# Identity multiplications on TensorE ahead of the first scores and among the packing steps of batch 0

## The chip, the cores and the metric

The kernel runs on one core of a Trainium2 chip, as one program. The metric is device microseconds of one execution, lower is better; the median of three runs of the kernel before is 1284.42 us (1284.23 to 1290.81).

## The reference, cut to what matters

Attention with packed keys comes first, for 8 batches of 8 heads, 576 tokens and head size 64: 32 pack rows `p` per head attend to `k`, `v`, and then the tokens `q` attend to the 32 packed rows. After it comes a mixture of four experts over all 4608 tokens, dense, each a two-layer network with ReLU, weighted by normalised probabilities.

```python
p_packed = sm_attn(p, k, v)              # 32 pack rows against 576 keys
out = sm_attn(q, p_packed, p_packed)     # 576 tokens against 32 packed rows
x = out.transpose(0, 2, 1, 3).reshape(B * S, H * D)
p = domain_probs / (domain_probs.sum(-1, keepdims=True) + 1e-09)
for e in range(E):
    h = np.maximum(x @ w1[e], 0.0)
    out += p[:, e:e + 1] * (h @ w2[e])
```

All of it is fp32. The kernel does the large products as sums of rounded fp32 parts (a high and a low part of each operand, in a one-pass fp32 type), and the small ones of attention in plain fp32; the second expert product goes by seven block products in place of eight.

## The kernel before, in words

One batch and one half expert (512 of the hidden columns) make a unit of work, 64 units in all. Each unit has two stages: tokens times a folded first weight (packed rows times `w1`, so that attention's second product and the expert's first become one), and then seven block products with the second weight. From about the unit 2 on the program is a long, dense stream of multiplications on TensorE, with VectorE, ScalarE and GpSimd preparing operands beside it.

The head of the program has no such stream to hide in. Batch 0 is packed first, alone, in two row groups `g` = 0 and 1, each with its own generator `pack_unit` (line 144), advanced in turns by `wavefront` (line 736). A group goes through these steps: load `kt` (its keys) and then `vt`/`vr` (its values); `scores` (line 126) multiplies pack rows with keys into one PSUM tile, 8 calls in a fixed row, and then VectorE takes the maximum (line 175) and scales it (179), ScalarE takes the exponential (181), and VectorE works out the reciprocal of the sum (188, 189); five transposes turn the result (lines 198 and 199, issued by `tr` at line 74); 20 multiplications with the values (line 208, by `mm` at line 69); VectorE scales that by the reciprocal (216); one transpose (219); VectorE copies it into the block-diagonal tile `ppbd` (222). The order of program, hence of TensorE, is: scores 0, scores 1, transposes 0, transposes 1, values 0, values 1, last transpose 0, last transpose 1.

`first_tokens` (line 399) follows: 20 calls of token scores with `ppbd` (line 422), the fold of `ppbd` with four loaded quarters of `w1` (`wraw`, line 430), high and low parts of the fold on ScalarE, and then the token softmax of batch 0 on VectorE and ScalarE. It already has rows of identity multiplications at three places (`fill`, line 439, with the counts of `FILL`, line 38).

The order on each engine comes from a planner that simulates the program's times when it is built. `together` (line 76) takes it out of its hands for a list of multiplications: they stand on TensorE behind everything issued before them, in the order of the list, and everything issued later stands behind them. What `mm` and `tr` issue is free among itself between two such lists. All loads go through one queue, SP's, in the order of the program: `kt` twice, `vt` and `vr` twice, tokens, second-weight blocks, tokens, the four `wraw`, and more. An fp32 call of TensorE appears in the trace as two MATMUL and two LDWEIGHTS records, an fp32 transpose as one of each.

Of the kernel before, what the change touches and what calls it, by code (L numbers as in the profile page):

```python
# [16 lines left out]
P = 128  # L17
B, H, S, D = 8, 8, 576, 64
# [3 lines left out]
NG = NPAIR // 2  # L22
SB = B // 2
HS = S // 2
# [11 lines left out]
PLAIN = ["a11", "a12", "a21", "a22"]  # L36
NPROD = len(ORDER)
FILL = (2, 4, 3)


@with_exitstack
def attention_moe(ctx: ExitStack, tc: tile.TileContext, q, k, v, p, dp, w1, w2, out):
# [17 lines left out]
    def after(ins, prev):  # L60
        tc.add_manual_dep(ins, prev.name, nosync, reason="order on an engine")

    def on_pe(res):
        if order["last"] is not None:
            after(res.ins, order["last"])
        order["free"].append(res.ins)

    def mm(**kw):
        res = nc.tensor.matmul(**kw)  # L69
        on_pe(res)  # L70
        return res.ins

    def tr(**kw):
        on_pe(nc.tensor.transpose(**kw))  # L74

    def together(calls):

        for i, kw in enumerate(calls):
            ins = nc.tensor.matmul(**kw).ins  # L79
            for prev in order["free"] if i == 0 else []:  # L80
                after(ins, prev)
            if order["last"] is not None:
                after(ins, order["last"])
            order["last"] = ins
        order["free"] = []

    def dbl():
        return ps_dbl.tile([P, 2, 512], F32, name="dbl")

    ident = const.tile([P, P], F32, name="ident")  # L90
# [10 lines left out]
    def cols(b, hh):  # L101

        i = (hh + b) % 2
        return slice(i * NPK, (i + 1) * NPK)

    def hi_of(dst, src, eng):
        if eng is nc.scalar:
            return nc.scalar.copy(out=dst, in_=src)  # L108
        return eng.tensor_copy(out=dst, in_=src)
# [13 lines left out]
        )  # L123
        nc.scalar.dma_start(out=pnd.rearrange("e (p t) -> p e t", p=P), in_=pb)

    def scores(bs, g, stationary, moving):

        pss = {b: dbl() for b in bs}
        calls = []
        for c in range(2):  # L130
            for j in range(2):
                for hh in range(2):
                    for b in bs:
                        p0 = 2 * j * NPK + cols(b, hh).start
                        calls.append(dict(
                            out=pss[b][p0:p0 + NPK, c, 0:HS], lhsT=stationary(b, 2 * g + j, hh),
                            rhs=moving[b][hh * D:(hh + 1) * D, j, c * HS:(c + 1) * HS], start=True, stop=True,
                        ))
        together(calls)
        return pss  # L140

    pts = {}

    def pack_unit(bs, g, new, relief=False):
        nfull = S // P
        r = S - nfull * P
        kts = {}
        for b in bs:
            if g == 0:
                pts[b] = small.tile([P, NPAIR, NPK], F32, name="pt")  # L150
                nc.sync.dma_start(out=pts[b], in_=p[b])
            kts[b] = new(b, [P, 2, S], "kt")
            nc.sync.dma_start(out=kts[b], in_=k[b][:, 2 * g:2 * g + 2, :])
        yield

        def load_v(b):
            vt, vr = new(b, [P, nfull, 4 * D], "vt"), new(b, [P, 4 * D], "vr")
            nc.sync.dma_start(
                out=vt, in_=v[b, 0:nfull * P, g * 4 * D:(g + 1) * 4 * D].rearrange("(c p) d -> p c d", p=P),
            )  # L160
            nc.sync.dma_start(out=vr[0:r], in_=v[b, nfull * P:S, g * 4 * D:(g + 1) * 4 * D])
            return [vt[:, c, :] for c in range(nfull)] + [vr]

        vt = load_v(bs[0])
        yield
        pss = scores(bs, g, lambda b, pr, hh: pts[b][hh * D:(hh + 1) * D, pr, :], kts)
        a1s, rss = {}, {}
        for b in bs:
            nb = small.tile([P, 1], F32, name="nb")
            a1s[b] = new(b, [P, S], "a1")  # L170
            a1v, raw = a1s[b].rearrange("p (c s) -> p c s", c=2), pss[b][:, :, 0:HS]
            if relief:
                nc.scalar.copy(out=a1v, in_=raw)
                raw = a1v
            nc.vector.tensor_reduce(out=nb, in_=raw, axis=AX.XY, op=ALU.max)  # L175
            if relief:
                nc.scalar.mul(nb, nb, -SCALE)
            else:
                marks["bias", b, g] = nc.vector.tensor_scalar_mul(nb, nb, -SCALE).ins
            sm = small.tile([P, 1], F32, name="sm")  # L180
            marks["first", b, g] = nc.scalar.activation(
                out=a1v, in_=raw, func=AF.Exp, scale=SCALE, bias=nb, accum_out=sm
            ).ins
            rss[b] = small.tile([P, 1], F32, name="rs")
            if relief:
                nc.scalar.activation(out=rss[b], in_=sm, func=AF.Copy, bias=1e-9)
            else:
                nc.vector.tensor_scalar_add(rss[b], sm, 1e-9)
            nc.vector.reciprocal(out=rss[b], in_=rss[b])
        yield  # L190
        prs = slice(2 * g, 2 * g + 2)
        for b in bs:
            if b != bs[0]:
                vt = load_v(b)
            at = new(b, [P, len(SC), P], "at")
            ps = dbl()
            for c in range(nfull):
                tr(out=ps[:, 0, c * P:(c + 1) * P], in_=a1s[b][:, c * P:(c + 1) * P], identity=ident)
            tr(out=ps[0:r, 1, 0:P], in_=a1s[b][:, nfull * P:S], identity=ident)
            turn = nc.vector if (b, g) == (0, 0) else nc.scalar  # L200
            hi_of(at[:, 0:nfull, :], ps[:, 0].rearrange("p (c s) -> p c s", s=P), turn)
            marks["turned", b, g] = hi_of(at[0:r, nfull, :], ps[0:r, 1, 0:P], turn).ins
            yield
            ps = dbl()
            for c, (_, n) in enumerate(SC):
                for h in range(4):
                    p0 = h // 2 * 2 * NPK + cols(b, h % 2).start
                    mm(
                        out=ps[p0:p0 + NPK, 0, 0:D], lhsT=at[0:n, c, p0:p0 + NPK],
                        rhs=vt[c][0:n, h * D:(h + 1) * D], start=c == 0, stop=c == len(SC) - 1,  # L210
                    )
            ppn = small.tile([P, D], F32, name="ppn")
            if relief:
                nc.scalar.mul(ppn, ps[:, 0, 0:D], rss[b])
            else:
                nc.vector.tensor_scalar_mul(ppn, ps[:, 0, 0:D], rss[b])
            yield
            ps = dbl()
            tr(out=ps[0:D, 0, 0:P], in_=ppn, identity=ident)
            psv = ps[0:D, 0, 0:P].rearrange("p (j n) -> p j n", j=2)  # L220
            for hh in range(2):
                hi_of(
                    ppbd[b % 4][hh * D:(hh + 1) * D, prs, cols(b, hh)], psv[:, :, cols(b, hh)],
                    nc.scalar if relief else nc.vector,
                )
            yield
# [172 lines left out]
    def first_tokens(pools, qts, raws, forms, grps):  # L399
# [93 lines left out]
        spare = turned[0][:, 0, cut:cut + P]  # L493
        fill(FILL[0], spare)
        for g in range(NG):
            then("ACT", hi_of(ghls[g][:, 0, :], fold[:, g, :], nc.scalar))
            less(fold[:, g, :], ghls[g][:, 0, :])
        for g in range(NG):
            then("ACT", nc.scalar.copy(out=ghls[g][:, 1, :], in_=fold[:, g, :]))
        fill(FILL[1], spare)  # L500
        shifted(1)
        powers(1)
        parts = turn(0)
        fill(FILL[2], fold[:, 0, 0:P])
        for ts, x in parts:
# [247 lines left out]
    def drain(gen):  # L753
        for _ in gen:
            pass
# [5 lines left out]
    with ExitStack() as first:  # L761
        pools = [first.enter_context(tc.tile_pool(name=f"unit{u}", bufs=1)) for u in range(NG)]

        def unit_tile(u):
            return lambda b, shape, name: pools[u].tile(shape, F32, name=name)

        def form_tile(shape, name):
            if name == "b2":
                return st_tile(F32)[:, 0:2 * DM].rearrange("p (f d) -> p f d", f=2)
            return hpool.tile(shape, F32, name="ablk", bufs=6)  # L770

        packs = [pack_unit([0], g, unit_tile(g)) for g in range(NG)]
        forms = t_form(0, form_tile, {n: nc.gpsimd for n in ("t1", "t2", "t3", "t4")})
        norm_probs()
        for i in (0, 1, 0, 1):
            next(packs[i])
        loads = first_loads()
        qts = [next(loads)]
        next(forms)
        qts.append(next(loads))  # L780
        raws = w1_load(0)
        load_probs(0, 0)
        drain(wavefront(packs, 1))
        rest = first_tokens(pools, qts, raws, forms, ((0, 0), (0, 1), (1, 1), (1, 0)))
        raws = w1_load(1)
# [36 lines left out]
    for u, (sb, ch, b) in enumerate(units):  # L822
# [46 lines left out]
        for i in range(NPROD):  # L869
            product(u, i)  # L870
            n = i + LA
# [78 lines left out]
```

## Time and profile before

| | us |
|---|---|
| median of three runs | 1284.42 |
| the profiled execution, its own time | 1283.3 |
| its span | 1281.5 |
| TensorE busy (98% of the span) | 1259.4 |
| VectorE busy | 958.6 |
| GpSimd busy | 859.9 |
| ScalarE busy | 492.5 |
| first multiplication starts | 5.26 |

Busy times overlap, so they don't add up to the span. Times in the trace count from the start of the span; what lies around the span is 1.8 us in the profiled execution. The names PE and PEld are TensorE's multiplications and its weight loads, DVE is VectorE, ACT is ScalarE, POOL is GpSimd, SP is the queue of the loads.

### The profile page before, as it was taken

Reading aid. Unit: us, or ns where it says so; the run is one execution under the profiler, and the core shown is the slowest. Engines: PE = TensorE matmul, PEld = TensorE weight load, DVE = VectorE, ACT = ScalarE, POOL = GpSimd, SP = SyncE. Lnnn points to the kernel's source line nnn. Section 1 sums busy time; section 2 is a strip of 40 time slices with the busy share of each in tenths; the row PEclk is TensorE's granted clock in tenths of the full one; section 3 lists DMA queues with packets and bytes.
Section 4 is the critical chain, followed back from the end, with each engine's and each line's share of the span. In section 5 each row is a group of like instructions: output and inputs, shape, how many; then the busy total and the mean of one; then the engine's idle time right before and its main releaser. Section 6 shows DMA issues by size and latency. Waiting matters only on the chain.

```text
span 1281.5 us, 26882 instructions
## 1 busy us (share of the span) xinstructions
PE 1259.4 (98%) x10772; PEld 1174.3 (92%) x10772; DVE 958.6 (75%) x1302; ACT 492.5 (38%) x885; POOL 859.9 (67%) x570
## 2 busy tenths in 40 slices
PE   7999999999999999999999999999999999999998
PEld 5789998998999999999999999999999999999998
DVE  5776777899975667997777667799679567766776
ACT  3544545646334333333324423333323533332321
POOL 4878888798995554666578464476568755556565
PEclk9999999999999999999999999999999999999999
DMA  9885656544466544554355546433436443454562
GB/s 347 320 296 186 221 178 227 181 146 169 159 222 197 164 159 131 187 162 158 128 151 174 183 143 205 144 126 125 155 128 213 149 136 116 127 155 127 178 216 99
DMA packets 91707, 223.93 MB, mean 175 GB/s; under 512 B 9280, under 2 KB 32192, under 8 KB 91584
## 3 DMA queue, kind: packets, MB, share of 16 engines
q1 hardware_dynamic: 90768, 221.92, 52.2%
q8 instruction: 86, 1.41, 0.5%
q10 hardware_dynamic: 816, 0.30, 0.1%
q14 instruction: 37, 0.30, 0.1%
HBM read 183.31 MB, written 38.87 MB: 173 GB/s over the span
## 4 chain that ended last, share of the span: by engine, by line
PE 72%; POOL 12%; DVE 9%; issue 3%; ACT 2%; DMA 1%; SPq 0%; ACTq 0%; DVEq 0%; POOLq 0%
PE dbl L69 66%; POOL st L112 8%; PE dbl L79 5%; DVE sblk L582 2%; POOL acc L731 2%; DVE ghl L112 1%; DVE ablk L356 1%; DVE acc L700 1%; POOL tt L112 1%; ACT ghl L108 1%; PE dbl L74 1%; POOL xl L112 1%; POOL b L621 0%; DVE a L244 0%; DVE nb L175 0%
## 5 line engine op out<-in xcount | busy, mean ns | idle before, releaser
L69 PE MATMUL dbl<-st,tt 128*128 128x288 f32 x5388 | 766.1, 296 | 2.5 <-DVE ghl L112 1.4
L69 PEld LDWEIGHTS dbl<-st,tt 128*128 128x128 f32 x5388 | 724.7, 188 | 46.7 <-issue 24.9
L112 POOL TENSOR_TENSOR st<-sblk,st 128x576 fp32r<-128x576 f32 x252 | 398.1, 1588 | 232.8 <-ACT st L108 221.6
L69 PE MATMUL dbl<-xh,ghl 128*128 128x288 f32 x2016 | 409.2, 295 | 3.3 <-DVE ghl L112 3.3
L112 POOL TENSOR_TENSOR st<-ablk,st 128x576 fp32r<-128x576 f32 x193 | 292.4, 1519 | 139.8 <-ACT st L108 134.5
L700 DVE TENSOR_TENSOR acc<-dbl,acc 128x576 f32<-128x576 f32 x385 | 287.8, 751 | 104.5 <-PE dbl L69 103.9
L69 PEld LDWEIGHTS dbl<-xh,ghl 128*128 128x128 f32 x2016 | 322.6, 188 | 4.0 <-DVE ghl L112 4.0
L356 DVE SCALAR_TENSOR_TENSOR ablk<-dbl,pbt 128x576 f32<-128x576 f32 x256 | 192.2, 752 | 142.7 <-PE dbl L69 141.1
L69 PE MATMUL dbl<-xl,ghl 128*128 128x288 f32 x1008 | 296.7, 295 | 0.0
L108 ACT CAST st<-sblk 128x576 fp32r<-128x576 f32 x252 | 170.4, 676 | 279.9 <-DVE sblk L582 215.3
L108 ACT CAST st<-ablk 128x576 fp32r<-128x576 f32 x193 | 130.4, 676 | 256.0 <-PE dbl L69 226.1
L69 PEld LDWEIGHTS dbl<-xl,ghl 128*128 128x128 f32 x1008 | 189.1, 188 | 0.0
L582 DVE TENSOR_TENSOR sblk<-ablk 128x576 f32<-128x576 f32 x126 | 134.1, 1065 | 9.2
L108 ACT CAST ghl<-dbl 128x512 fp32r<-128x512 f32 x128 | 73.0, 588 | 112.8 <-DVE ghl L112 57.8
L112 DVE TENSOR_TENSOR ghl<-dbl,ghl 128x512 fp32r<-128x512 f32 x126 | 84.7, 687 | 20.3 <-ACT ghl L108 18.1
L582 DVE TENSOR_TENSOR sblk<-ablk,sblk 128x576 f32<-128x576 f32 x63 | 78.5, 1246 | 5.4
L79 PE MATMUL dbl<-wraw,ppbd 64*32 64x512 f32 x1024 | 69.1, 597 | 0.0
L112 POOL TENSOR_TENSOR tt<-b,tt 128x512 fp32r<-128x512 f32 x42 | 62.3, 1493 | 2.1 <-ACT tt L108 2.0
L582 DVE TENSOR_TENSOR sblk<-sblk,ablk 128x576 f32<-128x576 f32 x63 | 58.1, 923 | 1.2
L731 POOL TENSOR_TENSOR acc<-acc,acc 128x576 f32<-128x576 f32 x28 | 43.5, 1562 | 12.6 <-DVE acc L700 12.5
L698 ACT COPY acc<-dbl 128x576 f32<-128x576 f32 x56 | 35.9, 641 | 36.5 <-PE dbl L69 36.4
L79 PEld LDWEIGHTS dbl<-wraw,ppbd 64*32 64x32 f32 x1024 | 15.4, 105 | 21.4 <-issue 18.1
(115 smaller groups left out, 465.2 us busy)
## 6 DMA issues: line engine op xcount, KB each, us to landing
tt<-td SPq DMA_DIRECT2D x192, 512.0 KB, 4.3
wraw<-in_w SPq DMA_DIRECT2D x136, 256.0 KB, 3.6
td<-tt SPq DMA_DIRECT2D x56, 512.0 KB, 4.0
pbt<-pnd SPq DMA_DIRECT2D x32, 288.0 KB, 4.1
out<-acc SPq DMA_DIRECT2D x31, 288.0 KB, 2.3
kt<-in_k SPq DMA_DIRECT2D x14, 576.0 KB, 5.7
kt<-in_q SPq DMA_DIRECT2D x14, 576.0 KB, 6.2
vt<-in_v SPq DMA_DIRECT2D x15, 512.0 KB, 5.1
```

What stands on the lines that cost most here:

```text
L69: res = nc.tensor.matmul(**kw)
L74: on_pe(nc.tensor.transpose(**kw))
L79: ins = nc.tensor.matmul(**kw).ins
L108: return nc.scalar.copy(out=dst, in_=src)
L112: return eng.tensor_tensor(out=dst, in0=src, in1=hi.bitcast(F32), op=ALU.subtract)
L356: res = nc.vector.scalar_tensor_tensor(out=a, in0=ps[:, :, 0:HS], scalar=0.0, in1=pbt[b][:, c * HS:(c + 1) * HS].rearrange("p (o t) -> p o ...
L582: marks["sum", u, name] = nc.vector.tensor_tensor(out=t, in0=blk(x), in1=blk(y), op=op).ins
L698: nc.scalar.copy(out=accs[b, i], in_=psv)
L700: nc.vector.tensor_tensor(out=accs[b, i], in0=psv, in1=accs[b, i], op=ALU.add)
L731: eng.tensor_tensor(out=m[dst], in0=m[x], in1=m[y], op=op)
```

## The change

A tuple `WARM` holds eight counts. `idle(ps, n)` makes a list of n calls that multiply the identity matrix by itself, 128x128 in fp32, into a piece of a PSUM tile that nothing reads. `pack_unit` of batch 0 gets four counts per group, `WARM[g::NG]`: (14, 2, 0, 1) for group 0 and (0, 4, 0, 1) for group 1. The first count goes ahead of the score calls in their list, the second ahead of the five transposes, the third ahead of the multiplications with the values, the fourth ahead of the last transpose. The other batches keep zeros. In all 22 calls are added and nothing is removed.

```diff
+WARM = (14, 0, 2, 4, 0, 0, 1, 1)
...
+    def idle(ps, n):
+
+        return [dict(out=ps, lhsT=ident, rhs=ident, start=True, stop=True) for i in range(n)]
+
+    def scores(bs, g, stationary, moving, fill=0):
 
         pss = {b: dbl() for b in bs}
-        calls = []
+        calls = idle(pss[bs[0]][:, 1, HS:HS + P], fill)
...
+    def pack_unit(bs, g, new, relief=False, fill=(0, 0, 0, 0)):
...
+        pss = scores(bs, g, lambda b, pr, hh: pts[b][hh * D:(hh + 1) * D, pr, :], kts, fill[0])
...
             ps = dbl()
+            if fill[1]:
+                together(idle(ps[:, 1, P:2 * P], fill[1]))
             for c in range(nfull):
...
             ps = dbl()
+            if fill[2]:
+                together(idle(ps[:, 1, 0:P], fill[2]))
             for c, (_, n) in enumerate(SC):
...
             ps = dbl()
+            if fill[3]:
+                together(idle(ps[:, 1, 0:P], fill[3]))
             tr(out=ps[0:D, 0, 0:P], in_=ppn, identity=ident)
...
-        packs = [pack_unit([0], g, unit_tile(g)) for g in range(NG)]
+        packs = [pack_unit([0], g, unit_tile(g), fill=WARM[g::NG]) for g in range(NG)]
```

## Rows read from the trace of the kernel before

**Rows 1.** The page: busy time by engine, and DMA in 40 slices.
```profile
PE 1259.4 (98%) x10772; PEld 1174.3 (92%) x10772; DVE 958.6 (75%) x1302; ACT 492.5 (38%) x885; POOL 859.9 (67%) x570
...
DMA  9885656544466544554355546433436443454562
```

**Rows 2.** The chain that ended last, 0 to 50: start, length, what.
```profile
1.19 3.93 DMA kt<-in_k
...
5.26 2.18 PE dbl L79 x16
...
8.51 0.84 ACT a L181 x2
...
9.72 0.67 DVE nb L175
...
10.66 0.84 ACT a L181 x2
...
14.04 0.29 DVE ppn L216
...
14.78 6.76 PE dbl L79 x56
```

**Rows 3.** Timeline of PE in short windows, 5.0 to 9.6: start, length, instructions.
```profile
5.26 0.71 PE L79 MATMUL dbl<-kt,pt 64*32 64x288 f32 x4 [5.26 <-DMA kt<-in_k]
...
8.11 1.21 PE L79 MATMUL dbl<-kt,pt 64*32 64x288 f32 x8
...
8.59 0.73 PE L79 MATMUL dbl<-kt,pt 64*32 64x288 f32 x4
9.48 0.30 PE L74 MATMUL dbl<-ident,a 128*128 128x128 f32 x1 [0.17 <-ACT a L181]
```

**Rows 4.** Timeline of PE, the scores of batch 1's first group.
```profile
44.41 1.17 PE L79 MATMUL dbl<-xh,pt 64*32 64x288 f32 x16
```

**Rows 5.** Stretches: window, length, busy and counts per engine, granted clock (PEclk), DMA.
```profile
5.00:9.00 4.00, 3.74 (x32) 1.43 (x32) 0.91 (x2) 0.49 (x1) 0.00 (x0) 1.00 1.04 345
...
316.40:319.60 3.20, 3.20 (x16) 3.20 (x15) 3.20 (x6) 2.52 (x5) 2.61 (x3) 0.50 0.00 0
320.00:323.00 3.00, 3.00 (x24) 3.00 (x24) 1.52 (x2) 1.35 (x2) 3.00 (x3) 1.00 0.10 41
```

**Rows 6.** Timeline of PE, the three rows of identity multiplications already there.
```profile
21.45 0.71 PE L79 MATMUL dbl<-ident 128*128 128x128 f32 x4
...
23.72 1.05 PE L79 MATMUL dbl<-ident 128*128 128x128 f32 x8
...
25.40 0.83 PE L79 MATMUL dbl<-ident 128*128 128x128 f32 x6
```

**Rows 7.** Timeline of all engines, 0 to 24.
```profile
1.01 0.29 POOL masks.py:199 TENSOR_SCALAR_AFFINE_SELECT ident<-ident 128x128 f32<-128x128 f32 x1
...
7.08 0.29 PEld L79 LDWEIGHTS dbl<-kt,pt 64*32 64x32 f32 x8 [0.67 <-DMA kt<-in_k]
...
11.54 0.77 PE L74 MATMUL dbl<-ident,a 128*128 128x128 f32 x5 [1.33 <-ACT a L181]
...
13.90 0.30 PE L74 MATMUL dbl<-ident,ppn 128*64 128x128 f32 x1
...
14.24 0.92 DVE L109 COPY ppbd<-dbl 64x64 f32<-64x64 f32 x4
14.38 0.30 PE L74 MATMUL dbl<-ident,ppn 128*64 128x128 f32 x1 [0.18 <-DVE ppn L216]
...
14.78 4.65 PE L79 MATMUL dbl<-ppbd,kt 128*128 128x64 f32 x40
...
19.36 2.16 PE L79 MATMUL dbl<-wraw,ppbd 64*32 64x512 f32 x16
```

**Rows 8.** The tile wraw, 0 to 24: its loads, and issue to landing.
```profile
L288 SPq DMA_DIRECT2D wraw<-in_w x4: 328/386/433, 10.9 to 13.8; - x4
...
DMA to landing us min/median/max: 6.1/6.5/6.6
```

More of the change, by code (lines that the diff above doesn't have):

```diff
@@ L124, in norm_probs @@
         nc.scalar.dma_start(out=pnd.rearrange("e (p t) -> p e t", p=P), in_=pb)
-    def scores(bs, g, stationary, moving):
+    def idle(ps, n):
+        return [dict(out=ps, lhsT=ident, rhs=ident, start=True, stop=True) for i in range(n)]
+    def scores(bs, g, stationary, moving, fill=0):
         pss = {b: dbl() for b in bs}
-        calls = []
+        calls = idle(pss[bs[0]][:, 1, HS:HS + P], fill)
         for c in range(2):
@@ L142, in attention_moe @@
     pts = {}
-    def pack_unit(bs, g, new, relief=False):
+    def pack_unit(bs, g, new, relief=False, fill=(0, 0, 0, 0)):
         nfull = S // P
@@ L165, in pack_unit @@
         yield
-        pss = scores(bs, g, lambda b, pr, hh: pts[b][hh * D:(hh + 1) * D, pr, :], kts)
+        pss = scores(bs, g, lambda b, pr, hh: pts[b][hh * D:(hh + 1) * D, pr, :], kts, fill[0])
         a1s, rss = {}, {}
```

## The prediction

> **What bounds the kernel now.** I read the page first. TensorE is busy for 98% of the span, and the DMA engines are nearly full in the first slices [rows 1]. A kernel like that gains from an edit in its head only if it can start its dense stream sooner; so I went to the chain that ended last, up to 50 us. It does not run on TensorE alone: it starts with 3.93 us of the first key load, then 2.18 us of group 0's scores, ScalarE's exponential of group 0, VectorE's maximum of group 1, the exponential of group 1, the last VectorE scale at 14.04, and then 6.76 us of TensorE from 14.78 (token scores and fold) [rows 2]. The reader is to see that group 1's scores are not on it: VectorE takes group 1's maximum at 9.72, after group 0's exponential, while group 1's scores end at 8.59 + 0.73 = 9.32 [rows 3].
>
> Then the pace of TensorE. In the scores four records run side by side, and a new four starts each 0.48 us (8.11 to 8.59) from the first to the last four [rows 3]. The same 16 records for batch 1 take 1.17 us against 2.18 [rows 2, 4]. Half of 0.48 is 0.24, and 4 x 0.24 + 0.21 is 1.17: the first scores run at half speed. The granted clock stands at 1.00 for that stretch [rows 5], but the steps contradict it; I take it that nothing lower was recorded before the first entry. Where 0.50 is recorded, 316.4 to 319.6, TensorE starts 16 records in 3.2 us, against 24 in 3.0 us at 1.00 [rows 5]. So the first scores run at the 1.2 GHz level, all other stretches of the head at 2.4 GHz: the transpose at 9.48 takes the same 0.30 us as a fast one at 13.90 [rows 3, 7], and the 40 token-score records step by 4.65 / 40 = 0.116 us, close to the identity records below. The level rose between 8.59 and 9.48, after 3.3 to 4.2 us of unbroken multiplication from 5.26.
>
> **What the change adds.** Nothing is removed, no load is moved and no wait is added, except that calls stand on TensorE in front of others.
>
> *The 14 calls ahead of the first scores* are 28 records. Eight such records take 1.05 us, six take 0.83, four 0.71 [rows 6]; with 0.30 us for the last one to drain a step is (1.05 - 0.30) / 7 = 0.107, (0.83 - 0.30) / 5 = 0.106 and 0.137. I take 0.108 at the fast level and, by the ratio of the scores, 0.216 at the slow one. The identity is ready at 1.01 + 0.29 = 1.30 [rows 7]; I let them start at 1.40. All slow they end at 1.40 + 6.05 = 7.45, all fast at 1.40 + 3.02 = 4.42, before the keys land at 5.26. If the level rises after as much unbroken work as before (3.3 to 4.2 us, so 4.7 to 5.6; I take 5.4), some 18.5 records run slow (4.0 us) and 9.5 fast (1.03 us): they end at 6.43. That is 1.17 us past the moment at which the keys landed. The scores then run fast and end at 6.43 + 1.17 = 7.60, against 5.26 + 2.18 = 7.44: **+0.16 us**. The bounds: with the rise at 4.7 the row of calls ends near 6.08 and the sum is -0.19; all fast would be -1.0; all slow, with slow scores, +2.2. Group 1's keys let its scores start at 7.08 now [rows 7], before 7.40, so group 1's load adds nothing, and its scores end near 8.6, off the chain as now.
>
> *Two calls ahead of group 0's transposes* (4 x 0.108 = 0.43) run from about 8.4 to 8.8; the transposes wait for the exponential until 9.48 + 0.16. Hidden. *Four calls ahead of group 1's transposes* (0.86) run in the 1.33 us for which TensorE sits idle before 11.54 [rows 7]. Hidden with 0.47 to spare; at the slow level they would take 1.73 and stick out by 0.40.
>
> *One call ahead of each last transpose* (0.216 each). The first stands directly between the last multiplication with the values and group 0's last transpose, where TensorE does not wait now (13.90): that transpose comes 0.22 later. VectorE's copies at 14.24, which wait for it, and the token scores at 14.78 come later by as much. The second call ends near 14.45 on the old clock, and group 1's transpose stands at 14.38 after a wait of 0.18 [rows 7]: 0.07 late, with group 1's copies not needed until the second half of the token scores. **+0.22 us**; the bounds are 0 (VectorE's own scale at 14.04 holds the copies) and 0.43 (both on the path).
>
> *What takes it up again.* The token scores would start at 14.78 + 0.38. The fold that follows takes 2.16 us for 16 records [rows 7], though at the step of its kind (512 columns against the 288 that step by 0.24: 0.427 for four records) it needs 4 x 0.427 + 0.17 = 1.88. The 0.28 is a wait for `wraw`, whose four loads are issued from 10.9 to 13.8 and land 6.1 to 6.6 us later, the last near 20.1 [rows 8]. SP's queue is paced by DMA engines that are full (share 1.04, [rows 5]), not by TensorE. So a front that is up to 0.28 late costs nothing behind the fold, and a front that is early gains next to nothing. **-0.28 us.**
>
> The sum is 0.16 + 0.22 - 0.28 = +0.1 us. Behind the fold ScalarE's and VectorE's chain is as it was, and the rest shifts with it. Against the profiled execution's 1283.3 (1281.5 and 1.8 around it) that is 1283.4. The median of the runs is 1.1 above that execution, and I add the sum to the median: 1284.42 + 0.1 = **1284.5**.
>
> The Trainium skill (TensorE: Matmul & The Clock Gate, "What's actually happening") states that the number of slow matmuls at the start varies between runs of one kernel, and gives 6, 11 and 14 for one. One profile cannot show that here. If it holds, the timed runs of before may have met a later rise than the profiled one, which is the first rival; without it the time would be the sum above.
>
> **The rivals.**
>
> *The rise is usually later, and the change pulls it forward.* In the profiled run it came just as the scores ended. Had it missed them, TensorE would go on with short bursts and the 1.33 us gap, and might rise only inside the token scores. At the slow level these 40 records would take 4.65 us more, with the rise in their middle 2.3. The change, whose 14 calls begin 3.9 us earlier and whose small rows fill the gaps, saves that in such runs, less the 0.28: 1284.42 - 2.0 = 1282.4, at the utmost 1279.8. For it: the profiled execution is faster than all three timed runs (1283.3 against 1284.23 and more). Against it: 1 us is little, and the profile shows the early rise.
>
> *The row of calls itself is late.* If the level does not rise before 7.45, the scores wait for 28 slow records and run slow themselves: +2.19 + 0.22 - 0.28 = +2.1, so 1286.5, or 1286.9 with the 0.40 of the four calls. It decides from a rise later than about 5.1 on: from there on the scores end later than now. For it: the rows of identity multiplications there all run where the level is high already, so none shows a rise under them. Against it: under the scores the level rose after at most 4.2 us.
>
> *The planner sets another order.* Its simulated times shift by some tenths, and further back the multiplications between two lists, and the loads, may swap. By the rows a single stall or slow stretch is worth 1.3 (the gap before 11.54) to 1.6 us (3.2 us at half speed): with two of either sign 1281.5 to 1287.5, and I can't say which.
>
> *It does not do what it says*: the clock rises as planned, the scores are faster, and nothing of it arrives, since the fold waits for `wraw`. That is the forecast itself.
>
> **How the numbers follow.** Forecast 50% (its own range 1284.0 to 1285.6), later rise in before 24%, late row of calls 14%, other order 12%. The range 1281.0 to 1288.0 holds the first, four fifths of the second, nearly all of the third and two thirds of the fourth; what a run of its own adds (1290.81 was seen) is left out, some 15 to 20% in all. Within 0.5% means 1278.0 to 1290.8, which is about what a measurement here can tell from no change: the three mechanisms of the head lie inside, so 90%; faster 4% and slower 6% are for the tail of the first rival, the other order and a run like the slowest.
>
> **What would show it.** In the profile after: 28 identity records from about 1.4, with steps near 0.216 that turn to 0.107 between 4.7 and 5.6; the first scores starting near 6.4 and ending near 7.6 at 0.24 a step; 1.33 us of idle time before group 1's transposes nearly gone; the token scores starting near 15.2; the fold without its wait, ending within 0.3 us of 21.5. A fold ending before 21.2 would show that `wraw` is not the gate. An order of multiplications that differs after 40 us would show the fourth rival; a change over 3 us with an equal order would prove the whole account wrong.

## The result, and the profile after

The changed kernel takes 1292.36 us in the median of twelve runs (1287.98 to 1294.82), the kernel before 1284.28 in twelve runs beside it (1282.74 to 1290.81). The ratio is 1.0053, with a 95% interval of 1.0040 to 1.0067: slower by 6.8 us (5.1 to 8.6); it compares all the runs, and the medians lie further apart, 8.1 us, in part because two of the twelve runs before are late ones (1288.76 and 1290.81). The prediction was 1284.5 with a range up to 1288.0.

The profiled execution after took 1294.25 us, its span is 1292.5, against 1283.3 and 1281.5: 11.0 us more, so it lies on the late side of the runs. The page says little. Busy time and records per engine, and the granted clock in 40 slices:

```profile
PE 1268.1 (98%) x10816; PEld 1182.4 (91%) x10816; DVE 959.2 (74%) x1302; ACT 491.6 (38%) x885; POOL 858.6 (66%) x570
...
PEclk8999999999999999999999999999999999999999
```

TensorE has 44 records more than in [rows 1], that is 22 calls of two, and 8.7 us more of busy time. All 44 at the pace of [rows 6] would be 4.8. One digit of the clock line, the first, is an 8: something in the first 32 us ran at the 1.2 GHz level. The timeline of PE after, 0 to 30 (start, length, instructions, and the idle time before them with what ended it), answers to [rows 3, 7]:

```profile
1.36 5.47 PE L80 MATMUL dbl<-ident 128*128 128x128 f32 x28 [1.36 <-POOL ident masks.py:199]
6.76 2.14 PE L80 MATMUL dbl<-kt,pt 64*32 64x288 f32 x32
8.84 0.71 PE L80 MATMUL dbl<-ident 128*128 128x128 f32 x4
9.93 0.77 PE L75 MATMUL dbl<-ident,a 128*128 128x128 f32 x5 [0.39 <-ACT a L186]
10.54 1.06 PE L80 MATMUL dbl<-ident 128*128 128x128 f32 x8
11.43 0.71 PE L75 MATMUL dbl<-ident,a 128*128 128x128 f32 x5
...
14.38 0.27 PE L75 MATMUL dbl<-ident,ppn 128*64 128x128 f32 x1
14.91 2.42 PE L80 MATMUL dbl<-ppbd,kt 128*128 128x64 f32 x20 [0.26 <-PE dbl L75]
18.82 3.96 PE L80 MATMUL dbl<-ppbd,kt 128*128 128x64 f32 x20 [1.49 <-DMA kt<-in_q]
22.71 3.64 PE L80 MATMUL dbl<-wraw,ppbd 64*32 64x512 f32 x16
26.28 0.71 PE L80 MATMUL dbl<-ident 128*128 128x128 f32 x4
```

Up to 14.91 the head is what the change wants: 28 records, 32 score records at the fast pace (2.14 us for what took from 5.26 to 9.32 in [rows 3]), no gap ahead of group 1's transposes, and token scores 0.13 us later than in [rows 7]. Then the 40 records that ran in one piece there break in two. The second half of the token scores waits 1.49 us for a load of tokens (`kt<-in_q`), takes 3.96 us in place of 2.42, and the fold takes 3.64 in place of 2.16. It ends at 26.35, against 21.52: 4.83 late. The stretches of after say why (window, length, busy and counts of PE, PEld, DVE, ACT, POOL, then the granted clock, the DMA share and GB/s):

```profile
17.00:19.00 2.00, 0.52 (x5) 0.41 (x4) 1.60 (x2) 0.00 (x0) 1.52 (x2) 1.00 1.04 386
19.50:25.00 5.50, 5.50 (x28) 3.68 (x31) 2.08 (x5) 1.35 (x3) 3.77 (x3) 0.50 1.02 375
...
180.00:183.00 3.00, 3.00 (x13) 3.00 (x14) 0.00 (x0) 0.80 (x3) 2.41 (x2) 0.50 0.77 219
```

The granted clock drops from 1.00 to 0.50, the 1.2 GHz level, behind the wait, and stays there through the token scores and most of the fold. The same happens a second time at 180, some 165 us behind the last added call. To see where the time went I put the evictions (the copies of TensorE's results out of PSUM) of one kernel beside those of the other, counted from the start, and read how late each is: 4.87 us at 33 us, 6.94 at 84, 10.97 at 180, and 10.94 at the end. So there are three losses, and nothing after them: **4.9 us in the head, 2.1 between 45 and 84, 4.0 at 170 to 183**.

The chain of after, in the head and at the third loss (start, length, what; compare [rows 2]):

```profile
2.12 7.02 DMA vt<-in_v
...
9.57 9.11 DMA kt<-in_q
...
18.82 7.60 PE dbl L80 x36
...
174.49 4.53 DMA b<-in_w
...
179.57 0.32 ACT ppn L223
...
179.93 0.42 PE dbl L75
```

In the head it now runs over the second token load, which is not in [rows 2] at all. At the third loss it runs over a load of a second-weight block `b`, then ScalarE, then TensorE. ScalarE's and TensorE's timelines there, first of before:

```profile
169.52 0.62 ACT L108 CAST tt<-b 128x512 fp32r<-128x512 f32 x1 [2.36 <-DMA b<-in_w]
...
170.41 0.30 PE L74 MATMUL dbl<-ident,ppn 128*64 128x128 f32 x1 [0.56 <-ACT ppn L214]
```

and of after:

```profile
179.04 0.62 ACT L109 CAST tt<-b 128x512 fp32r<-128x512 f32 x1 [5.15 <-DMA b<-in_w]
...
179.93 0.42 PE L75 MATMUL dbl<-ident,ppn 128*64 128x128 f32 x1 [3.13 <-ACT ppn L223]
```

ScalarE's cast of the block stands ahead of the small `ppn` scale on which TensorE's transpose depends. The load lands late, the cast waits 5.15 us in place of 2.36, the transpose 3.13 in place of 0.56, and then the level is at 0.50 for a while: 2.6 us of waiting, and the remaining 1.4 lie in the slow stretch. The middle loss is in the waits of TensorE, 45 to 90 (who waits for whom: total, times, longest), before:

```profile
PE dbl L74 <- ACT a L181: 1.0, 1, 1.0
PE dbl L69 <- ACT at L108: 0.8, 1, 0.8
```

and after:

```profile
PE dbl L70 <- ACT at L109: 1.4, 1, 1.4
PE dbl L70 <- DVE ghl L113: 1.2, 1, 1.2
PE dbl L80 <- DVE acc L711: 1.1, 2, 0.9
PE dbl L75 <- ACT a L186: 1.0, 1, 1.0
```

The wait for `ghl` is in before too, 1.1 us, a little ahead of this window; without it 1.8 us became 3.5, which is 1.7 of the 2.1. TensorE's own order is the same apart from the added calls, but the planner gave the other engines another one between about 24 and 65 us: casts of second-weight blocks moved behind copies of results on ScalarE, block sums on VectorE and GpSimd changed places, stores of prepared weights moved past loads on SP.

### The profile page after: what moved, and what is told of

Same layout as the page of the kernel before. It is cut to its first block, busy times and chain, and to the rows that moved or that the text cites. A ratio compares the mean times of both kernels' runs of the same rounds, so it can differ in the third digit from the quotient of the medians.

```text
span 1292.5 us, 26969 instructions
## 1 busy us (share of the span) xinstructions
PE 1268.1 (98%) x10816; PEld 1182.4 (91%) x10816; DVE 959.2 (74%) x1302; ACT 491.6 (38%) x885; POOL 858.6 (66%) x570
## 4 chain that ended last, share of the span: by engine, by line
PE 69%; DVE 13%; POOL 11%; issue 3%; DMA 2%; ACT 2%; SPq 0%; ACTq 0%; DVEq 0%; POOLq 0%
PE dbl L70 63%; POOL st L113 7%; PE dbl L80 5%; DVE sblk L593 3%; POOL acc L742 2%; DVE acc L711 2%; DVE ablk L367 2%; DVE ghl L113 2%; POOL tt L113 1%; DMA vt<-in_v 1%; PE dbl L75 1%; ACT ghl L109 1%; DMA kt<-in_q 1%; DVE a L255 1%; DVE a L281 1%
```

## The experiments

There are three suspects, one for each loss: the wait for the second token load and the level behind it; the other order on the helping engines; and a late load at 170, whose tie to the change was unknown. Medians are against runs of the kernel before on the same chip. Every kernel computes the whole output; added calls write what nothing reads.

To hold the order still while calls come and go, a list of positions is tied together, neighbour by neighbour, on VectorE, ScalarE, GpSimd and SP (`log` holds each engine's instructions as the program issued them). "Old order" means that of before from about 24 us on, "changed order" that of after. Ahead of 24 us the kernels with the 14 calls keep an order of VectorE that the change brought: group 1's maximum stands ahead of group 0's reciprocal.

```diff
+PINNED = {"vector": [...], "scalar": [...], "gpsimd": [...], "sync": [...]}
...
+    for key, seq in PINNED.items():
+        for i, j in zip(seq, seq[1:]):
+            after(log[key][j], log[key][i])
```

### The change again, the order without the rows, the rows without the order

The change, unaltered:

> The changed kernel as it is, for a second trace of it. Its first trace is 11 us behind the kernel before in three places: 4.9 us by the first stage (a wait of 1.5 us for the second token load at 17.3, then the 1.2 GHz level from 19.4 to 26.2), 2.1 us between 45 and 84, 4.0 us at 170 to 180. Theory A, the planner's order: the 2.1 us between 45 and 84 come again in every trace, since the order of loads and of VectorE, ScalarE and GpSimd differs there, and the head's wait differs from run to run. Theory B, the rows themselves: the wait for the second token load and the slow level behind it come again in every trace. Both expect 1290 to 1294 as the median.

The median is 1293.47 against 1283.82, ratio 1.0068 (1.0053 to 1.0083). Its profile has the same three losses: 4.2 by 33 us, 2.1 more by 84, 3.1 more by 180; a wait of 1.1 us for the token load, the level at 0.50 from 18.9 to 25.7. They belong to the kernel, not to one execution.

The kernel before, without any added call, tied to the changed order:

> The kernel before, without any identity row, with the changed kernel's order of loads and of instructions on VectorE, ScalarE and GpSimd forced on it by edges. Theory A expects 1286 to 1290 (2.1 us between 45 and 84, perhaps the 4.0 us at 170 too). Theory B expects no change, 1283 to 1285.

The median is 1286.42, ratio 1.0013 (1.0003 to 1.0023). The head is 0.06 late, 2.1 more are lost between 45 and 84, and at 170 the wait is the old one (0.57). Its waits of TensorE, 45 to 90, are three of the four of after:

```profile
PE dbl L98 <- ACT at L61: 1.4, 1, 1.4
PE dbl L108 <- DVE acc L61: 1.1, 2, 0.9
PE dbl L103 <- ACT a L61: 1.0, 1, 1.0
```

So of the three losses the middle one comes with the order, and only that one.

All 22 calls, tied to the old order:

> The changed kernel with all 22 calls, with the order of before on all engines forced back from about 24 us on (the maximum of group 1 stays ahead of group 0's reciprocal). Theory A expects 1283 to 1286: with the order the loss goes. Theory B expects 1288 to 1293: wait and slow level in the head stay.

The median is 1289.07, ratio 1.0036 (1.0019 to 1.0053). Nothing is lost between 45 and 84. At 170 the wait is 3.36 and 5.3 us are lost. In the head this one profile shows a wait of 0.6 for the token load, no fall of the level, and ends 0.66 late. By the ratios the order is the smaller part; the rows by themselves cost more.

### Which rows

```diff
-WARM = (14, 0, 2, 4, 0, 0, 1, 1)
+WARM = (14, 0, 0, 0, 0, 0, 0, 0)
```

> As the last one, but with the 14 calls ahead of the first scores alone; the eight small ones are gone. Theory A expects 1283 to 1286. Theory B expects the wait for the second token load as well, 1288 or more, unless the small rows cause it; then 1283 to 1285.

The 14 calls alone, old order: 1287.01, ratio 1.0016 (1.0002 to 1.0029). The twelve runs fall in two heaps, five from 1283.1 to 1284.8 and seven from 1286.9 to 1289.2, which is a switch and not a smear: the granted clock over the whole execution is 0.998 to 1.000 in the five and 0.995 to 0.997 in the seven. The profiled one (1287.13) shows the late branch; of the early one there is no trace. Its timeline of PE, and a stretch:

```profile
14.10 2.42 PE L109 MATMUL dbl<-ppbd,kt 128*128 128x64 f32 x20
17.97 3.83 PE L109 MATMUL dbl<-ppbd,kt 128*128 128x64 f32 x20 [1.46 <-DMA kt<-in_q]
...
174.34 0.30 PE L104 MATMUL dbl<-ident,ppn 128*64 128x128 f32 x1 [0.57 <-ACT ppn L62]
```

```profile
19.50:25.00 5.50, 5.50 (x27) 2.70 (x26) 3.05 (x6) 0.54 (x2) 3.77 (x3) 0.50 1.04 390
```

The token scores begin 0.7 us earlier than before. How much of that the calls bring is open: e2 and e12, without a call but with VectorE's changed order in the head, begin them at 14.15 and 14.71. Then the load is late, and the level is at 0.50 from 18.7 to 25.5. The head is 3.9 us late. At 170 all is as before.

```diff
-WARM = (14, 0, 2, 4, 0, 0, 1, 1)
+WARM = (0, 0, 2, 4, 0, 0, 1, 1)
```

> The eight small calls (2 and 4 ahead of the transposes, 1 and 1 ahead of the last ones) without the 14, in the order of before. All traces so far with the small calls have a stall of 3 us at 170 to 180 for a second-weight load, all without them 0.6 us. Theory C, the small calls bring that stall: 1285.5 or more, and a wait of 3 us there in the trace. Theory D, chance of the load: 1283 to 1284.5, like before, since the head without the 14 calls has its old pace.

The eight small calls alone, old order: 1283.71 against 1284.07, ratio 0.9996 (0.9983 to 1.0009). Eleven runs lie between 1283.4 and 1284.6. The profiled one, at 1289.01, is the exception: a wait of 3.82 at 170, the level at 0.50 behind it. So the small rows cost nothing as a rule, and a late load at 170 can come, rarely, without the 14 calls.

### The second token load earlier

```diff
-        qts = [next(loads)]
+        qts = [next(loads), next(loads)]
...
-        qts.append(next(loads))
```

This issues the second token load right behind the first, ahead of the second-weight blocks. With the 14 calls and the old order:

> The 14 calls alone, in the order of before, with the second token load issued directly behind the first, ahead of the three second-weight loads. Theory B2 (the row is paid for by TensorE's wait for that load at 16.5 to 18, and by the 1.2 GHz level that follows such a wait): the wait goes, and all runs lie near the fast half of the 14 calls alone, 1281.5 to 1283.5, with a granted clock of 0.998 or more. Its rival (the rows slow all loads, and the next one takes the wait's place, the four w1 loads): 1285 to 1289 with clocks of 0.995 to 0.997 as without the move.

The median is 1283.74 against 1284.07, ratio 0.9992 (0.9977 to 1.0006). There is no wait and no fall. The timeline of PE and the stretch:

```profile
15.00 4.65 PE L109 MATMUL dbl<-ppbd,kt 128*128 128x64 f32 x40
```

```profile
19.50:25.00 5.50, 4.78 (x35) 2.68 (x34) 4.61 (x6) 3.56 (x7) 4.25 (x4) 1.00 1.01 373
```

The 40 records run in one piece again. That takes the head's loss away, but the 1283.7 is no gain over before: the 1281.5 to 1283.5 that I had expected was missed, narrowly. The earlier load by itself, without any call:

> The kernel before with the second token load issued early, no identity row. Theory B2 expects 1283 to 1284, no change: TensorE does not wait for that load before, by 0.2 us. Its rival (the load is worth something by itself) expects 1282 or less.

The median is 1283.99, ratio 0.9998 (0.9986 to 1.0010). It is worth nothing alone. What it does in e6 is to take away the loss that the 14 calls brought in.

The other way round, the load left late and the wait filled, so that TensorE does not stand still:

```diff
+            if g == 0:
+                mms(idle(ps[:, nt * P:(nt + 1) * P], 8))
```

> The 14 calls alone, in the order of before, and 8 more identity calls (1.7 us at the fast level) between the two halves of the token scores, where TensorE waits for the second token load. If the cost is the slow level that follows the wait, the level stays high and the median falls from 1287.0 to 1283 to 1284.5. If the cost is the wait itself or what comes with it, 1286 to 1288 stays.

The median is 1287.62, ratio 1.0023 (1.0013 to 1.0034). Timeline of PE:

```profile
14.28 2.42 PE L109 MATMUL dbl<-ppbd,kt 128*128 128x64 f32 x20
16.53 2.00 PE L109 MATMUL dbl<-ident 128*128 128x128 f32 x16
18.47 2.42 PE L109 MATMUL dbl<-ppbd,kt 128*128 128x64 f32 x20
...
173.18 0.30 PE L104 MATMUL dbl<-ident,ppn 128*64 128x128 f32 x1 [2.09 <-ACT ppn L62]
```

```profile
19.50:25.00 5.50, 4.74 (x36) 2.69 (x36) 4.73 (x7) 2.94 (x5) 3.31 (x3) 1.00 1.04 386
```

The level holds, and the second half takes its 2.42 us. So in this kernel the slow pace hung on the idle time. The time was not returned, and the median stayed where it was: the filling ends as late as the load did, which leaves 1.3 us in the head, and a wait of 2.09 appeared at 170 that e4, with eight calls less, does not have.

### All together, with the load repaired; the order taken apart

All 22 calls, early load, old order:

> All 22 calls, the second token load issued directly behind the first, the order of before otherwise. If the changed kernel's loss is the sum of the wait for that load (with the slow level behind it) and the planner's order, and of nothing else, both are gone: 1283 to 1284.5, with clocks of 0.998 or more in most runs. If all 22 calls together cost something else (the run of all calls with the old order was at 1289.1, the 14 alone at 1287.0): 1285.5 or more.

The median is 1287.95 against 1284.41, ratio 1.0023 (1.0009 to 1.0037). The head is 0.15 us ahead of before. In its place 1.1 us are lost between 33 and 45, where TensorE waits for a quarter of the next first weight, which before does not (its waits, 0 to 45):

```profile
PE dbl L109 <- DMA wraw<-in_w: 1.5, 1, 1.5
```

At 170 the transpose waits 2.50, and 1.9 us are lost. So the rows still cost something with the token load repaired, and the late load at 170 is the larger part of what this trace shows of it, not the whole. The profiled execution (1286.27) is the second fastest of the twelve; where the others lose 1.7 us more in the median no trace shows.

The change with the early load, changed order:

> The changed kernel in its own order, with only the second token load issued early. By the same sum the order's 2.1 to 2.5 us stay and the rest goes: 1286 to 1287, against 1292.4 to 1293.5 without the move. If the order and the slow level are tied in another way: 1288 or more.

The median is 1289.34, ratio 1.0027 (1.0013 to 1.0042): the head is 0.25 ahead, 2.1 are lost between 45 and 84, and the wait at 170 is 2.03. In the trace two losses out of three are left, as they should be. The median is not as it should be: 1286 to 1287 had been expected. The profiled execution (1286.30) is the fastest of the twelve, and what the others lose besides, 3.0 us in the median, is in no trace.

The kernel before with the changed order on SP only, and on VectorE, ScalarE and GpSimd only:

> The kernel before with the changed order of the loads and stores on SP's queue alone, between its 33rd and 55th entry. Order alone cost 2.15 us in the trace between 45 and 84 and 1286.4 as a median. If the loads' order carries it: 1286 to 1287. If the order on VectorE, ScalarE and GpSimd does: 1283 to 1284.5.

> The kernel before with the changed order on VectorE, ScalarE and GpSimd, and the old order on SP's queue. The complement of the one before: 1286 to 1287 if these engines carry the 2.15 us, 1283 to 1284.5 if the loads do; if both differ from 1284 each carries a part.

The medians are 1284.51, ratio 0.9999 (0.9984 to 1.0014), and 1286.59, ratio 1.0012 (1.0000 to 1.0025). The second loses 2.0 us by 84 and has the same three waits as e2. By the ratios the loads' order costs nothing that these runs can tell, and the engines' order carries the loss, though both intervals of it (e2, e12) reach down to 1.0003 and less.

The traces are less clear than the ratios. All five in the changed order lose 2.1 us between 45 and 84 (after, e1, e2, e10, e12). But of the thirteen traces with the old order on the engines only seven lose nothing there. e6 and e11 lose 1.2 us, with a wait of 0.9 for `acc` that is also one of the waits of after; e16 and e17 0.7 and 1.0 behind a load; e9 the 1.1 named above; and e18, further down, 3.7. So a loss there can come without the changed order; with it, it came every time.

### What ties 170 us to the head

The waits of that transpose, gathered, looked as if they went by how many calls there are, not by what the calls do. So the calls were made nearly empty, 32 columns of weights against one column of data, at the same places and in the old order:

```diff
-        return [dict(out=ps, lhsT=ident, rhs=ident, start=True, stop=True) for i in range(n)]
+        return [dict(out=ps[0:32, 0:1], lhsT=ident[:, 0:32], rhs=ident[:, 0:1], start=True, stop=True) for i in range(n)]
```

> The kernel before in its own order with 22 added calls at the places of the change, each of 32 weight columns and one data column, so that they take hardly any time. Theory E, the place of TensorE's code: 22 more calls move the fetches of its code, and one falls upon the second-weight load at 170, which lands late: the stall there is in the trace (2 to 3.5 us against 0.6), median 1285.3 to 1287. Theory F, the stall comes from the work of the calls in the head (another pace of what follows): no stall, 1283 to 1284.5. Both: the second token load lands 7.5 us after its issue, as without rows, if it is the rows' work that slows it.

The median is 1288.79 against 1283.59, ratio 1.0035 (1.0016 to 1.0055), all twelve runs above 1286.5. Timeline of PE:

```profile
1.36 1.66 PE L109 MATMUL dbl<-ident 128*32 128x1 f32 x28 [1.36 <-POOL ident masks.py:199]
5.21 3.55 PE L109 MATMUL dbl<-kt,pt 64*32 64x288 f32 x32 [2.20 <-DMA kt<-in_k]
...
176.45 0.30 PE L104 MATMUL dbl<-ident,ppn 128*64 128x128 f32 x1 [1.97 <-ACT ppn L62]
```

The 14 calls end at 3.0 and delay nothing; still the transpose at 170 waits 1.97, the `b` load landing 4.8 us after its issue (3.3 before). The head is late by 4.65 here, for a reason of its own: the level rose at 8.1, fell at 11.5, rose, and was at 0.50 again from 18.4 to 25.2.

All 22 calls, early load, old order, and 32 nearly empty calls ahead of them (16 in the later kernel e18):

```diff
+        if fill:
+            spare = pss[bs[0]][0:32, 1, HS + P:HS + P + 1]
+            calls = [dict(out=spare, lhsT=ident[:, 0:32], rhs=ident[:, 0:1], start=True, stop=True) for i in range(32)] + calls
```

> As the run with all 22 calls, the early token load and the old order (1288.0, stall of 2.5 us at 170), with 32 more tiny calls ahead of the first row, 54 more than before in all. Theory E: the fetch of code moves on by more than half of its period of some 15 us, past that load; the stall is 0.6 us and the median 1283 to 1285. Theory F: 1287 to 1289 and the stall stay.

The median is 1287.0, ratio 1.0016 (1.0002 to 1.0030): above the 1283 to 1285 that went with a moved place of the code, at the lower end of the rival's 1287 to 1289. The execution that was profiled took 1719 us, so its trace can't be set beside the others, and the 32 calls delay the row behind them by an unknown time. The run is inconclusive.

Nearly empty calls only, 22, 38 and 54 of them, all ahead of the first scores, old order, the load where it was:

```diff
-WARM = (14, 0, 2, 4, 0, 0, 1, 1)
+WARM = (22, 0, 0, 0, 0, 0, 0, 0)
```

> The kernel before in its own order with 22 tiny calls (32 weight columns, one data column), all ahead of the first scores, where TensorE waits for the keys until 5.2, and none among the packing steps. Theory E (the number of TensorE's instructions brings the stall at 170): the stall is 2 us or more, median 1285 to 1287, now without the head's loss of the run with the calls spread. Theory G (what cost there was the calls standing between the packing steps): 1283 to 1284.5.

> The same with 38 tiny calls. Theory E: another place of the code, so another stall at 170: between 0.6 and 3.5 us, the median 1283 to 1287, and not the same as with 22. Theory G: 1283 to 1284.5.

> The same with 54 tiny calls, which are nearly a whole period of the code's fetches (64 such calls) on. Theory E: the place of the code is nearly that of before, the stall at 170 0.6 to 1 us, the median 1283 to 1284.5. Theory G: the same, 1283 to 1284.5; a stall of 2 us or more would speak against E.

The medians are 1289.57, ratio 1.0039 (1.0025 to 1.0054); 1285.1, ratio 1.0014 (1.0005 to 1.0023); 1284.85, ratio 1.0008 (0.9998 to 1.0018). More calls cost less, though the first and the last lie above what was expected. Their heads are late: in its trace the kernel with 22 by 7.0 us, the level being at 0.50 from 12.3 to 29.4, and the one with 54 by 1.8. The transpose at 170 with 22:

```profile
180.55 0.30 PE L104 MATMUL dbl<-ident,ppn 128*64 128x128 f32 x1 [2.51 <-ACT ppn L62]
```

with 38:

```profile
171.45 0.30 PE L104 MATMUL dbl<-ident,ppn 128*64 128x128 f32 x1 [0.57 <-ACT ppn L62]
```

and with 54, where the calls last until 7.2 and push the scores:

```profile
173.35 0.30 PE L104 MATMUL dbl<-ident,ppn 128*64 128x128 f32 x1 [0.76 <-ACT ppn L62]
```

The last run puts it to the test with the work in place: the 22 calls of the change, early load, old order, and 16 nearly empty calls, 38 in all.

> All 22 calls of the change, the early token load and the old order (1288.0 with a stall of 2.5 us at 170), with 16 tiny calls ahead of the first row, so that 38 calls are added in all, the number at which the tiny calls alone showed a stall of 0.6 us. They delay the first row by up to 0.9 us. Theory E: the stall is 1 us or less and the median 1283.5 to 1285.5, so that the three parts (order, token load, place of the code) are the whole loss. If the work of the calls brings the stall as well: 2 us or more there and 1287 to 1289.

The median is 1286.21 against 1283.55, ratio 1.0012 (0.9997 to 1.0026).

```profile
176.31 0.30 PE L104 MATMUL dbl<-ident,ppn 128*64 128x128 f32 x1 [0.53 <-ACT ppn L62]
```

The wait is gone, as forecast. The median is above the 1283.5 to 1285.5 that I had given. The 16 calls delay the first row by 2.2 us where I had reckoned 0.9 (first scores at 8.81, the head 2.3 late), which is most of it. This trace is that of the second slowest run (1288.98) and loses 3.7 us more between 45 and 84, in the old order, with the level at 0.50 from 55.9 to 59.3. So the three parts are not all that can go wrong here.

The wait of that transpose in every profile, by the number of calls added:

| calls added | kernels | wait, us |
|---|---|---|
| 0 | before, e2, e7, e11, e12 | 0.56, 0.57, 0.53, 0.69, 0.50 |
| 8 | e5 (one run of twelve like it) | 3.82 |
| 14 | e4, e6 | 0.57, 0.70 |
| 22 | after, e1, e3, e8, e9, e10, e13, e15 | 3.13, 2.08, 3.36, 2.09, 2.50, 2.03, 1.97, 2.51 |
| 38 | e16, e18 | 0.57, 0.53 |
| 54 | e17 | 0.76 |

All eight profiles with 22 calls have it, with or without work in the calls, in the old order or the changed one, with the load early or late; of the eleven others only that one run of e5. What is shown, with one trace of each kernel, is that the wait goes with the number of calls added to TensorE. By which path a number of calls makes a load some 150 us later land 1.2 to 2.8 us late is not shown. The order on SP's queue beside it is not the difference: in before and in seven of the eight traces with 22 calls the store ahead of it is issued 0.37 us before it and the next one 1.4 us behind it. One coincidence points somewhere: the page lists two DMA queues of instructions, of which I take the larger for TensorE's (it has 21544 of the 26882 instructions of before). Its packets of 16 KB come one each 10 to 18 us at this place, and more calls shift when. In before such a packet follows the issue of the `b` load by 9.4 us. In eight of the nine traces with the wait, that of e5 among them, it starts between 0.1 us ahead of the issue and 2.6 behind it, and in no trace without the wait: the nearest there are 2.9 and 3.1 behind (e4, e6) and 2.6 ahead (e18). The ninth, e3 with 3.9, does not fit, and no run moved the packet by itself. That stays open.

## Why the prediction was wrong

**The sum of the head held up to the token scores, in part by luck.** The level was forecast to rise between 4.7 and 5.6; the first record of the granted clock in the trace of after is at 5.75, a little later. The scores were to begin at 6.43 and begin at 6.76. Group 1's transposes lost their 1.33 us of idle time. The token scores were forecast at 15.16 (+0.38) and came at 14.91 (+0.13): VectorE now takes group 1's maximum ahead of group 0's reciprocal and group 1 comes sooner, which the forecast did not have and which made up for the later scores.

**The step that failed is "What takes it up again".** It named `wraw` as the only gate on the way to the fold, never asked for the load that the second half of the token scores needs, and took the loads to be paced "not by TensorE" ("no load is moved"). In before that load is issued at 9.27 and lands at 16.8; with the 0.14 us that after shows between landing and start it is usable at 16.9, and it is needed at 14.78 + 20 x 0.116 = 17.1. So the stream that [rows 7] show as one piece of 40 had 0.2 us to spare in its middle. Asking would not have been enough: a forecast start at 15.16 needs the load at 17.5, later than 16.9. It is the load that moved. Issues at 9 to 10 and the us from issue to landing, before and after:

```profile
kt<-in_q SPq DMA_DIRECT2D x1, 576.0 KB, 7.5
kt<-in_q SPq DMA_DIRECT2D x1, 576.0 KB, 9.1
```

After the change it is issued at 9.57, 0.3 later, and takes 1.6 us longer, so it lands at 18.7. Why it takes longer was not found. e4, e6 and e8 show the rest: TensorE waits 1.5 us, the level falls behind the wait, and the second half and the fold take 1.54 and 1.48 us longer (3.96 for 2.42, 3.64 for 2.16); with the load early both are gone; with the wait filled only the pace comes back. Between the medians of e4 and e6 lie 3.3 us.

The Trainium skill (TensorE: Matmul & The Clock Gate, "Why this matters for your kernels") advises against idle gaps between bursts of matmuls, and means longer ones than that of the head. These traces differ: the level fell behind the 1.49 us here. Nor does the length of a gap decide by itself: the 1.33 us ahead of group 1's transposes in [rows 7] left the level at 1.00, and at the same place it fell to 0.50 behind 1.05 us in e13 and 1.39 in e15.

**"Behind the fold ScalarE's and VectorE's chain is as it was" failed twice.** Once by a rival, the planner's other order: its mechanism was right, TensorE's order is the same and the helpers' is not, and it got 12%. Its size was good too (two events of 1.3 to 1.6; measured 2.1 in the trace and 1.7 by the ratio of e2). And once by something that stood nowhere: the late load at 170, tied to the number of calls, behind which eight traces lose 1.4 to 5.3 us. The prediction said that a change over 3 us with an equal order would prove the whole account wrong. e3 is that case, with 4.6.

**The account.** By ratios: order 1.0013 (e2), head 1.0016 (e4, over both of its heaps), load at 170 with what else e9 loses 1.0023 (e9), together 1.0052, against 1.0053 for the change and 1.0068 for the same kernel in e1. Each has an interval of some 0.001 to each side, so the close agreement is luck in good part; e3 (head and 170: 1.0039 by this sum, 1.0036 measured) and e10 (order and 170: 1.0036, 1.0027 measured) lie within their intervals. That the three losses are there is shown by the traces; that they are the whole is not, since the medians of e9 and e10 lie 1.7 and 3.0 us above the runs whose traces were read.

**The rivals.** The late row of calls is not in after, but e6 came near it: there the row of 28 records takes 6.03 us, next to the 6.05 of "all slow", and its scores, at the fast pace, end at 9.46, 0.14 later than in [rows 3]. In e4, e9 and after the same row takes 5.13, 5.22 and 5.47. The first record of the clock is at 6.92 in e6 and between 4.70 (e10) and 5.75 (after) in seven more traces with this row, so the rise moves by up to 2.2 us from one execution to the next. The Trainium skill (TensorE: Matmul & The Clock Gate, "What's actually happening") states, as the prediction cited, that the number of slow matmuls at the start varies between runs of one kernel. These rows agree. Whether some timed runs of before have a later rise than the profiled one, the first rival, they cannot say. The six traces without calls ahead of the first scores have it between 8.28 (e2) and 10.93 (e12), all well ahead of the token scores; e7, with 10.05, begins those 0.06 later than before. The 2.0 us that the rival would give lie inside the interval of e6 (down to 0.9977, which is 3.0 us) and are not in its median. "It does not do what it says" was right about the gain: where the rise is early and all else is repaired, the heads of e9 and e10 are 0.15 and 0.25 us ahead, and nothing of that can be measured at the end.

No version here beats the kernel before; of those with the 14 calls at work e6 equals it.

## What to carry to other kernels

Before filling a head with warm-up work, list every load that the first dense stream consumes, with its landing and the time at which its first reader is due; a stream that looks unbroken may have a load in its middle that is on time by 0.2 us. A wait that follows can cost twice, once as idle time and once as slow pace: here 1.5 and 3.0 us. And where a planner sets the order, or the program is made longer in front, compare the order of all engines and the waits far behind the edit before crediting or blaming the edit itself.

## What the runs showed of the hardware

- The level fell from 1.00 to 0.50 behind waits of 1.1 to 1.5 us for the token load (after, e1, e4) and not behind waits of 0.4, 0.5 and 0.6 at the same place (e2, e11, e3). Ahead of group 1's transposes it fell behind 1.05 and 1.39 us (e13, e15) and not behind 1.33 (before) and 1.31 (e11). At 170 it fell in or behind waits of 3.1 to 3.8 (after, e3, e5) and of 2.08 (e1), and not behind waits of 1.97 to 2.51 (e8, e9, e10, e13, e15). The price in the head was 3.0 us of slow pace in after, twice the wait.
- The second token load landed 7.5 us after its issue in all kernels without calls ahead of the first scores that were read for it (before, e2, e5, e11, e12), and 7.9 to 9.1 in nine with such calls (after, e1, e3, e4, e8, e13, e15, e16, e17), whether the calls do work or next to none. Why was not found.
- Calls of next to no work did not bring the rise forward. With 22 of them ahead of the scores (e15) the first record of the clock is at 8.9, against 5.75 with the 14 of the change; with 54 of them (e17), on TensorE without a break from 1.36 to 7.2, the 32 score records still take 4.06 us, as in before, and the first record is at 12.6.
